# k and q of the last six steps transposed by DMA instead of TensorE

## The chip, the cores and the metric

The kernel runs on one core of one Trainium2 chip. Time is device microseconds (us) of one execution. Most executions of one kernel agree closely, but some fall into a slower state, a few per cent longer. Each run carries its state, "slow" when it is over 1.5% above the fastest run of the same kernel. A profiled execution has a span, from first to last instruction, which is about 1.8 us less than the run's time.

Engines: PE is TensorE, PEld its weight loads, DVE is VectorE, ACT is ScalarE, POOL is GpSimd, SP is SyncE. SPq and ACTq are the DMA issues of SyncE and ScalarE. L12 is line 12 of the kernel profiled, so the same statement has another line number in another kernel.

## The reference

```python
# attention with decay: B=4, H=8, S=768, D=64
intra = (q k^T * lam**(i-j) for i>=j) v                # inside a block
inter = (q * lam**(i+1)) @ state                        # what earlier blocks left
state = lam**block * state + (k * lam**(block-1-j))^T v
# then, on x = attention output as (B, S, 512):
h = relu(x @ w_in); u, v = halves of h (512 each)
v_n = (v - mean) / sqrt(var + 1e-6)
out = (u * (w_spatial @ v_n + b_spatial)) @ w_out
```

## The kernel before

There are 12 steps of 256 tokens (three per batch, numbered 0 to 11). For a step n the program has short names: `lk` loads k, q and v, `c` casts them on GpSimd, `T` transposes k and q, `A` computes the scores, `K` the new state, `O` the output of attention. `pv`, `pu`, `pvs`, `po` are the matmuls of the gated MLP (multilayer perceptron); batch 1's `pv` and `pu` run beside steps 5 to 7. The order on TensorE, GpSimd and SyncE is as written in the texts below. On ScalarE and VectorE a scheduler chooses it.

```python
def cast_part(s, n, part):
    if part == "k":      # product with the decay ldec: two inputs
        nc.gpsimd.tensor_tensor(out=kd..., in0=s["k_in"], in1=ldec..., op=ALU.mult)
    elif part == "q":    # plain cast
        nc.gpsimd.tensor_copy(out=qc..., in_=s["q_in"])
    ...
def trans_step(n):
    pt = two_banks([P, 2, NG, T2], f"pt_{n}", BF16)
    for j, src in ((0, kd), (1, qc)):
        for g in range(NG):
            for c in range(2):                      # 16 transposes of 128x128
                nc.tensor.transpose(out=pt[:, j, g, c * P:(c + 1) * P], in_=src..., identity=ident)
    nc.scalar.activation(out=kT, in_=pt[:, 0], func=AF.Copy)
    nc.vector.tensor_tensor(out=qT..., in0=pt[:, 1], in1=lq, op=ALU.mult)   # decay of q
...
def kv_step(n):                                     # the state; sd has two SBUF inputs
    nc.vector.tensor_tensor(out=sd, in0=prev, in1=lb, op=ALU.mult)
    nc.vector.tensor_tensor(out=s_sb[:, c], in0=sd, in1=pkv[:, c], op=ALU.add)
...
def pv(b, r):                                       # matmuls into ps, then
    nc.scalar.activation(out=vh[:, pair, :], in_=ps, func=AF.Relu)
    ... bn_stats, bn_aggr (VectorE), rstd (ScalarE), reciprocal, vn (VectorE)
...
run("""... c:5 lk:7 pvs:0:0 pvs:0:1 T:3 pvs:0:2 A:3 K:3 c:6 pvs:0:3 T:4 po:0:0
    A:4 O:3 K:4 po:0:1 c:7 po:0:2 lk:8 T:5 pv:1:0
    A:5 O:4 K:5 pu:1:0 lk:9 T:6 pv:1:1 pu:1:1""")
```

Of the kernel before, what the change touches and what calls it, by code (L numbers as in the profile page):

```python
# [9 lines left out]
FP32 = mybir.dt.float32  # L10
BF16 = mybir.dt.bfloat16
I32 = mybir.dt.int32  # L12
AF = mybir.ActivationFunctionType
ALU = mybir.AluOpType
# [4 lines left out]
def kernel(  # L19
# [12 lines left out]
    nc = tc.nc  # L32
    P = 128
    B, H, S, D = q.shape
# [4 lines left out]
    NG = H // 2  # L39
    NCH = DM // P  # L40
    NR = S // (2 * P)
    NS = B * NR
    T2 = 2 * P
    HW_ = S // 2

    const = ctx.enter_context(tc.tile_pool(name="const", bufs=1))
    wpool = ctx.enter_context(tc.tile_pool(name="wpool", bufs=1))
    fin = ctx.enter_context(tc.tile_pool(name="fin", bufs=4))
    att = ctx.enter_context(tc.tile_pool(name="att", bufs=3))
# [10 lines left out]
    st = {}  # L60

    def load_v(n, eng, blocks=(0, 1)):
        b, r = divmod(n, NR)
        toks = slice(r * T2, (r + 1) * T2)
        if "v_in" not in st[n]:
            st[n]["v_in"] = fin.tile([P, H, 2, D], FP32, tag="v_in", name=f"v_in_{n}")
        v_in = st[n]["v_in"]
        for c in blocks:
            eng.dma_start(out=v_in[:, :, c, :],  # L69
                          in_=v[b, :, toks][:, c * P:(c + 1) * P].rearrange("h p d -> p h d"))  # L70
# [32 lines left out]
    qpos_i = const.tile([P, 2, 2, D], I32)  # L103
    nc.gpsimd.iota(qpos_i, pattern=[[1, 2], [0, 2], [2, D]], base=1, channel_multiplier=0)

    rel_i = const.tile([P, 2, D], I32)
    nc.gpsimd.iota(rel_i, pattern=[[1, 2], [2, D]], base=0, channel_multiplier=-1)
    ident = const.tile([P, P], BF16)
# [3 lines left out]
    nc.vector.tensor_copy(out=krev, in_=krev_i)  # L112
    qpos = const.tile([P, T2], FP32)
    nc.vector.tensor_copy(out=qpos, in_=qpos_i.rearrange("p m a d -> p (m a d)"))
    causal = const.tile([P, P], FP32)
    nc.vector.tensor_scalar(out=causal, in0=rel_i.rearrange("p m d -> p (m d)"), scalar1=0,
                            scalar2=None, op0=ALU.is_ge)
# [5 lines left out]
    loglam = const.tile([P, H], FP32)  # L123
# [13 lines left out]
    with tc.issue_after(last.ins):  # L137
        load_v(0, nc.scalar, (1,))
        load_v(1, nc.scalar, (0,))
    l128 = const.tile([P, NG], FP32)  # L140
    nc.scalar.activation(out=l128, in_=logl, func=AF.Exp, scale=float(P))
    sq_t = const.tile([P, 1], FP32)
# [32 lines left out]
    def cast_step(n, parts=("k", "q", "v")):  # L175
        s = st[n]
        for part in parts:
            cast_part(s, n, part)

    def cast_part(s, n, part):  # L180
        if part == "k":
            kd = s["kd"] = att.tile([P, 2, H, D], BF16, tag="kd", bufs=4, name=f"kd_{n}")
            nc.gpsimd.tensor_tensor(out=kd.rearrange("p c h d -> p h c d"), in0=s["k_in"],  # L183
                                    in1=ldec.unsqueeze(2).unsqueeze(3).broadcast_to((P, H, 2, D)),
                                    op=ALU.mult)
        elif part == "q":
            qc = s["qc"] = att.tile([P, 2, H, D], BF16, tag="qc", bufs=4, name=f"qc_{n}")
            nc.gpsimd.tensor_copy(out=qc.rearrange("p m h d -> p h m d"), in_=s["q_in"])  # L188
        else:
            vc = s["vc"] = att.tile([P, H, 2, D], BF16, tag="vc", bufs=4, name=f"vc_{n}")  # L190
            nc.gpsimd.tensor_copy(out=vc, in_=s["v_in"])  # L191

    def trans_step(n):
        kd, qc = st[n]["kd"], st[n]["qc"]
        pt = two_banks([P, 2, NG, T2], f"pt_{n}", BF16)
        for j, src in ((0, kd), (1, qc)):
            for g in range(NG):
                for c in range(2):
                    nc.tensor.transpose(  # L199
                        out=pt[:, j, g, c * P:(c + 1) * P],  # L200
                        in_=src[:, c, 2 * g:2 * g + 2, :].rearrange("p h d -> p (h d)"),
                        identity=ident)
        kT = att.tile([P, NG, T2], BF16, tag="kT", name=f"kT_{n}")
        nc.scalar.activation(out=kT, in_=pt[:, 0], func=AF.Copy)  # L204
        qT = att.tile([P, NG, 2, 2, D], BF16, tag="qT", name=f"qT_{n}")
        nc.vector.tensor_tensor(out=qT.rearrange("p g m a d -> p g (m a d)"), in0=pt[:, 1],  # L206
                                in1=lq, op=ALU.mult)
        st[n]["qT"], st[n]["kT"] = qT, kT

    def qblk(n, g, hh, c):  # L210
        return st[n]["qT"][hh * D:(hh + 1) * D, g, :, c, :]

    def scores_step(n):


        kT = st[n]["kT"]
        a_sb = att.tile([P, 2, 2, 2, 2, P], BF16, tag="a_sb", bufs=2, name=f"a_{n}")
        st[n]["a"] = a_sb
        for i in range(2):
            pam = two_banks([P, 2, 2, 2, P], f"pam_{n}_{i}")  # L220
            for g2 in range(2):
                for c in range(2):
                    for hh in range(2):
                        g = 2 * i + g2
                        nc.tensor.matmul(out=pam[:, hh, g2, c, :],  # L225
                                         lhsT=kT[hh * D:(hh + 1) * D, g, c * P:(c + 1) * P],
                                         rhs=qblk(n, g, hh, c), start=True, stop=True)
            nc.vector.tensor_tensor(  # L228
                out=a_sb[:, i].rearrange("p h g c x -> p (h g) c x"),
                in0=pam.rearrange("p h g c x -> p (h g) c x"),  # L230
                in1=amask[:, i].rearrange("p h g x -> p (h g) x").unsqueeze(2)
                .broadcast_to((P, 4, 2, P)), op=ALU.mult)
# [143 lines left out]
    def wt_piece(s):  # L376
        ps = two_banks([P, 2, 1024], f"pwt_{s}", BF16)
        for j in range(2):
# [7 lines left out]
    acts = {"c": cast_step, "T": trans_step, "A": scores_step, "K": kv_step, "O": out_step,  # L386
            "lk": load_step, "pv": pv, "pu": pu, "pvs": pvs,
            "po": po, "wt": wt_piece, "win": load_win, "wsp": load_wsp, "wout": load_wout,
            "mask": make_amask, **{"c" + x: lambda n, x=x: cast_step(n, (x,)) for x in "kqv"}}

    def run(text):
        for word in text.split():
# [6 lines left out]
        T:0 K:0 A:0 T:1 O:0 K:1 A:1 pv:0:0 O:1 T:2 K:2 pv:0:1 A:2 pu:0:0 O:2  # L399
        c:4 pu:0:1 wt:0 pv:0:2 wt:2 pu:0:2 wt:4  # L400
        c:5 lk:7 pvs:0:0 pvs:0:1 T:3 pvs:0:2 A:3 K:3 c:6 pvs:0:3 T:4 po:0:0
        A:4 O:3 K:4 po:0:1 c:7 po:0:2 lk:8 T:5 pv:1:0
        A:5 O:4 K:5 pu:1:0 lk:9 T:6 pv:1:1 pu:1:1
    """)
    for n in range(2 * NR - 1, NS):
        b, r = divmod(n, NR)
        a = b - 1
        more = n + 1 < NS
        run((f"A:{n + 1} " if more else "") + f"O:{n}" + (f" K:{n + 1}" if more else ""))
        nxt = ""  # L410
        if n + 3 < NS:
            nxt += f" c:{n + 3}"
        if n + 5 < NS:
            nxt += f" lk:{n + 5}"
        if n + 2 < NS:
            nxt += f" T:{n + 2}"
        if n == 2 * NR - 1:
            run(f"pv:{b}:2 {nxt} pu:{b}:2")
        elif r == 0:
            run(f"pvs:{a}:0 pvs:{a}:1 {nxt} pvs:{a}:2 pvs:{a}:3")  # L420
        elif r == 1:
            run(f"po:{a}:0 po:{a}:1 {nxt} po:{a}:2 pv:{b}:0")
        elif more:
            run(f"pv:{b}:1 pu:{b}:0 pv:{b}:2 {nxt} pu:{b}:1 pu:{b}:2")
        else:
            run(f"pv:{b}:1 pv:{b}:2 pu:{b}:0 pu:{b}:1 pu:{b}:2")
# [31 lines left out]
```

## Time and profile before

The profile on which the prediction rests came from a run of 182.71 us, while the timed runs took 176.49 to 177.64.

| | profile of the slow run (used to predict) | profile of a fast run |
|---|---|---|
| span | 180.9 us | 174.4 us |
| scores of step 5 start | 74.79 | 72.67 |
| scores of step 7 start | 91.81, after a wait of 1.28 | 88.86, after a wait of 0.45 |
| scores of step 8 start | 108.23 | 101.70 |
| scores of step 8 to the end | 72.7 | 72.7 |

Two more places of the fast run will be needed, the first loads on SyncE and the first sd on VectorE:

```profile
0.74 1.07 SPq L78 DMA_DIRECT2D k_in<-in_k_dram  x2
1.86 1.12 SPq L80 DMA_DIRECT2D q_in<-in_q_dram  x1
```

```profile
17.36 1.94 DVE L254 TENSOR_TENSOR sd<-s,l 128x256 f32<-128x256 bf16 x1
...
91.63 0.72 DVE L325 TENSOR_SCALAR vn<-vh,mv,rstd 128x512 bf16<-128x512 bf16 x2
```

### The profile page before, as it was taken

What the parts mean: (1) busy time and instruction counts of PE and PEld (TensorE: products, weight loads), DVE (VectorE), ACT (ScalarE), POOL (GpSimd) and SP (SyncE); (2) the same over time, 40 slices, a digit from 0 to 9 for tenths busy, and PEclk for the clock granted to TensorE, in tenths of its full rate; (3) what the DMA queues carried; (4) which work ended last, traced back from release to release, by engine and by line L of the source; (5) the groups of instructions that cost most, each with busy time, mean ns of one, the idle gap of its engine ahead of it and who ended that gap; (6) DMA issues with size and microseconds to landing.
All of it is one profiled execution on the core that took longest, in us unless ns stands there. A gap on an engine that the chain in (4) does not pass through costs nothing.

```text
span 180.9 us, 3629 instructions
## 1 busy us (share of the span) xinstructions
PE 145.4 (80%) x1528; PEld 95.2 (53%) x1540; DVE 106.0 (59%) x182; ACT 77.3 (43%) x88; POOL 53.2 (29%) x50
## 2 busy tenths in 40 slices
PE   0041699399869999997955999999999999999890
PEld 0031566176636665676742655567866645776430
DVE  0712988921652889579998447179994713834400
ACT  2940057237911045677450014756822257660051
POOL 2439639400555566207556702000000000000000
PEclk9999999969987999999997899999999999999997
DMA  3999999999999999999899900630000026000036
GB/s 79 266 224 239 212 243 224 194 202 200 239 226 218 253 216 270 321 263 196 220 238 224 236 5 0 235 116 4 0 4 0 0 104 248 0 0 5 0 126 222
DMA packets 68497, 28.36 MB, mean 157 GB/s; under 512 B 50560, under 2 KB 65536, under 8 KB 68480
## 3 DMA queue, kind: packets, MB, share of 16 engines
q1 hardware_dynamic: 62560, 24.25, 58.2%
q0 software_dynamic: 2512, 2.95, 9.4%
q10 hardware_dynamic: 3408, 0.92, 2.7%
q8 instruction: 12, 0.20, 0.5%
q14 instruction: 5, 0.04, 0.1%
HBM read 24.78 MB, written 6.29 MB: 172 GB/s over the span
## 4 chain that ended last, share of the span: by engine, by line
PE 53%; DVE 17%; DMA 12%; SPq 9%; ACT 3%; issue 1%; POOL 1%; ACTq 0%; POOLq 0%
PE pvs L344 17%; PE po L359 10%; DMA wsp_raw<-in_moe_w_spatial_dram 8%; PE pv L313 8%; PE pu L334 7%; SPq L78 5%; DVE a L228 5%; DMA v_in<-in_v_dram 5%; DVE vn L325 4%; PE pvs L346 3%; PE pt L199 3%; DVE gT L348 2%; SPq L80 2%; DVE st L319 2%; SPq L69 2%; DVE sd L254 2%
## 5 line engine op out<-in xcount | busy, mean ns | idle before, releaser
L344 PE MATMUL pvs<-wt_sb,vn 128*128 128x384 bf16 x192 | 39.8, 343 | 5.2 <-DVE vn L325 5.1
L228 DVE TENSOR_TENSOR a<-pam,amask 128x1024 bf16<-128x1024 f32 x24 | 28.5, 1211 | 3.4 <-PE pam L225 3.4
L183 POOL TENSOR_TENSOR kd<-k_in,ldec 128x1024 bf16<-128x1024 f32 x12 | 23.0, 1917 | 23.2 <-DMA k_in<-in_k_dram 16.2
L344 PEld LDWEIGHTS <-vn 128*128 128x128 bf16 x192 | 19.4, 103 | 19.6 <-DVE vn L325 6.3
L204 ACT ACTIVATE kT<-pt 128x1024 bf16<-128x1024 bf16 x12 | 12.2, 1021 | 38.9 <-PE pt L199 38.9
L348 DVE TENSOR_TENSOR gT<-pvs,uT 128x768 bf16<-128x768 f32 x16 | 15.3, 957 | 19.6 <-PE pvs L346 19.6
L334 PE MATMUL pu<-xT,win_sb 128*128 128x256 bf16 x192 | 24.0, 284 | 2.9 <-DMA win_sb<-in_moe_w_in_dram 2.9
L313 PE MATMUL pv<-win_sb,xT 128*128 128x512 bf16 x89 | 22.0, 380 | 1.9 <-ACT xT L288 1.6
L359 PE MATMUL po<-wout_sb,gT 128*128 128x512 bf16 x91 | 21.7, 379 | 1.4 <-DVE a L228 0.7
L319 DVE BATCH_NORM_STATS2 st<-vh 128x6 f32<-128x512 bf16 x24 | 15.4, 682 | 12.5 <-ACT vh L316 12.3
L334 PEld LDWEIGHTS <-win_sb 128*128 128x128 bf16 x192 | 19.2, 102 | 6.6 <-DMA win_sb<-in_moe_w_in_dram 3.0
L288 ACT ACTIVATE xT<-pat 128x1024 bf16<-128x1024 f32 x12 | 15.8, 1320 | 15.6 <-PE pat L285 15.4
L191 POOL CAST vc<-v_in 128x1024 bf16<-128x1024 f32 x12 | 12.8, 1066 | 28.1 <-DMA v_in<-in_v_dram 20.9
L372 ACT ACTIVATE o<-po 128x1024 f32<-128x1024 f32 x11 | 11.3, 1025 | 18.3 <-PE po L359 18.3
L336 ACT ACTIVATE uT<-pu 128x1024 bf16<-128x1024 f32 x12 | 12.2, 1021 | 10.1 <-PE pu L334 10.1
L316 ACT ACTIVATE vh<-pv 128x1024 bf16<-128x1024 f32 x12 | 12.2, 1021 | 8.2 <-PE pv L313 8.1
L199 PE MATMUL pt<-ident,kd 128*128 128x128 bf16 x96 | 8.2, 234 | 9.1 <-POOL kd L183 9.1
L359 PEld LDWEIGHTS <-gT 128*128 128x128 bf16 x96 | 9.1, 98 | 11.7 <-DVE gT L348 1.3
L313 PEld LDWEIGHTS <-xT 128*128 128x128 bf16 x96 | 8.9, 98 | 11.3 <-ACT xT L288 2.0
L188 POOL CAST qc<-q_in 128x1024 bf16<-128x1024 f32 x12 | 12.9, 1076 | 5.9 <-DMA q_in<-in_q_dram 5.7
L206 DVE TENSOR_TENSOR qT<-pt,lq 128x1024 bf16<-128x1024 bf16 x12 | 8.2, 684 | 10.7 <-ACT kT L204 10.7
L325 DVE TENSOR_SCALAR vn<-vh,mv,rstd 128x512 bf16<-128x512 bf16 x24 | 14.1, 629 | 0.3
(54 smaller groups left out, 142.0 us busy)
## 6 DMA issues: line engine op xcount, KB each, us to landing
k_in<-in_k_dram SPq DMA_DIRECT2D x24, 256.0 KB, 5.3
q_in<-in_q_dram SPq DMA_DIRECT2D x12, 512.0 KB, 6.7
out_dram<-o SPq DMA_DIRECT2D x11, 512.0 KB, 3.1
v_in<-in_v_dram SPq DMA_DIRECT2D x21, 256.0 KB, 6.5
wsp_raw<-in_moe_w_spatial_dram POOLq DMA_DIRECT2D x1, 1152.0 KB, 14.2
win_sb<-in_moe_w_in_dram POOLq DMA_DIRECT2D x2, 512.0 KB, 8.2
v_in<-in_v_dram ACTq DMA_DIRECT2D x3, 256.0 KB, 6.3
wout_sb<-in_moe_w_out_dram POOLq DMA_DIRECT2D x1, 512.0 KB, 17.4
```

Source lines behind the costliest of these rows:

```text
L183: nc.gpsimd.tensor_tensor(out=kd.rearrange("p c h d -> p h c d"), in0=s["k_in"], in1=ldec.unsqueeze(2).unsqueeze(3).broadcast_to((P, H, 2, ...
L188: nc.gpsimd.tensor_copy(out=qc.rearrange("p m h d -> p h m d"), in_=s["q_in"])
L199: nc.tensor.transpose(out=pt[:, j, g, c * P:(c + 1) * P], in_=src[:, c, 2 * g:2 * g + 2, :].rearrange("p h d -> p (h d)"), identity=ident)
L228: nc.vector.tensor_tensor(out=a_sb[:, i].rearrange("p h g c x -> p (h g) c x"), in0=pam.rearrange("p h g c x -> p (h g) c x"), in1=amask[: ...
L288: nc.scalar.activation(out=xT[b][:, r].rearrange("p g (c d m) -> p (g c) m d", c=2, m=2), in_=po.rearrange("p g c (m d) -> p (g c) m d", m ...
L313: nc.tensor.matmul(out=ps[:, j], lhsT=x[:, r, c, j * P:(j + 1) * P], rhs=win_sb[:, c, DH:DFF], start=(c == 0), stop=(c == NCH - 1))
L319: nc.vector.bn_stats(out=m["st6"][:, t, :], in_=vh[:, t, :])
L325: nc.vector.tensor_scalar(out=m["vn"][:, t, :], in0=vh[:, t, :], scalar1=mv[:, t, 0:1], scalar2=rstd[:, t:t + 1], op0=ALU.subtract, op1=AL ...
L334: nc.tensor.matmul(out=ps[:, f], lhsT=win_sb[:, c, f * P:(f + 1) * P], rhs=x[:, r, c, :], start=(c == 0), stop=(c == NCH - 1))
L344: nc.tensor.matmul(out=ps[:, i, 0:HW_], lhsT=m["vn"][:, s, f * P:(f + 1) * P], rhs=wt_sb[:, s, cols], start=(s == 0), stop=False)
L348: nc.vector.tensor_tensor(out=m["gT"][:, f, :].rearrange("p (i x) -> p i x", i=2), in0=ps[:, :, 0:HW_], in1=m["uT"][:, f, :].rearrange("p ...
L359: nc.tensor.matmul(out=ps[:, j], lhsT=gT[:, c, t * P:(t + 1) * P], rhs=wout_sb[:, c, :], start=(c == 0), stop=(c == NCH - 1))
```

## The change

The intent: TensorE is the busiest engine, and 16 of its instructions a step only transpose. For steps 6 to 11 a DMA does it, from SBUF to SBUF, requested on SyncE's queue. The decay of q, which the removed VectorE product carried, moves into the q cast on GpSimd. kT and qT get five buffers instead of three.

```diff
+    NPE = 6
...
+    lqt = const.tile([P, 2, H], FP32)          # decay of q by token and head
...
-            nc.gpsimd.tensor_copy(out=qc..., in_=s["q_in"])
+            if n < NPE:
+                nc.gpsimd.tensor_copy(out=qc..., in_=s["q_in"])
+            else:
+                nc.gpsimd.tensor_tensor(out=qc..., in0=s["q_in"], in1=lqt..., op=ALU.mult)
...
+    def dma_trans(n):
+        kT = att.tile([P, 2, NG, P], BF16, tag="kT", bufs=5, name=f"kT_{n}")
+        qT = att.tile([P, 2, NG, P], BF16, tag="qT", bufs=5, name=f"qT_{n}")
+        for dst, src in ((kT, st[n]["kd"]), (qT, st[n]["qc"])):
+            nc.sync.dma_start_transpose(out=dst..., in_=src...)
...
     def trans_step(n):
+        if n >= NPE:
+            return
...
-        A:4 O:3 K:4 po:0:1 c:7 po:0:2 lk:8 T:5 pv:1:0
-        A:5 O:4 K:5 pu:1:0 lk:9 T:6 pv:1:1 pu:1:1
+        A:4 O:3 K:4 po:0:1 c:7 po:0:2 lk:8 dt:6 T:5 pv:1:0
+        A:5 O:4 K:5 pu:1:0 lk:9 dt:7 pv:1:1 pu:1:1
...
+        if n + 3 < NS:
+            nxt += f" dt:{n + 3}"              # behind lk:{n + 5}
```

More of the change, by code (lines that the diff above doesn't have):

```diff
@@ L104 @@
     nc.gpsimd.iota(qpos_i, pattern=[[1, 2], [0, 2], [2, D]], base=1, channel_multiplier=0)
+    tpos_i = const.tile([P, 2], I32)
+    nc.gpsimd.iota(tpos_i, pattern=[[1, 2]], base=1, channel_multiplier=2)
     rel_i = const.tile([P, 2, D], I32)
@@ L114 @@
     nc.vector.tensor_copy(out=qpos, in_=qpos_i.rearrange("p m a d -> p (m a d)"))
+    tpos = const.tile([P, 2], FP32)
+    nc.vector.tensor_copy(out=tpos, in_=tpos_i)
+    nc.vector.tensor_scalar(out=tpos[D:P, :], in0=tpos[D:P, :], scalar1=-float(P), scalar2=None,
+                            op0=ALU.add)
     causal = const.tile([P, P], FP32)
@@ L139 @@
         load_v(1, nc.scalar, (0,))
+    lqt = const.tile([P, 2, H], FP32)
+    with tc.issue_after(last.ins):
+        for m in range(2):
+            nc.scalar.activation(out=lqt[:, m, :], in_=loglam, func=AF.Exp,
+                                 scale=tpos[:, m:m + 1])
     l128 = const.tile([P, NG], FP32)
@@ L187, in cast_part @@
             qc = s["qc"] = att.tile([P, 2, H, D], BF16, tag="qc", bufs=4, name=f"qc_{n}")
-            nc.gpsimd.tensor_copy(out=qc.rearrange("p m h d -> p h m d"), in_=s["q_in"])
+            if n < NPE:
+                nc.gpsimd.tensor_copy(out=qc.rearrange("p m h d -> p h m d"), in_=s["q_in"])
+            else:
+                nc.gpsimd.tensor_tensor(out=qc.rearrange("p m h d -> p h m d"), in0=s["q_in"],
+                                        in1=lqt.rearrange("p m h -> p h m").unsqueeze(3)
+                                        .broadcast_to((P, H, 2, D)), op=ALU.mult)
         else:
@@ L191, in cast_part @@
             nc.gpsimd.tensor_copy(out=vc, in_=s["v_in"])
+    def dma_trans(n):
+        kT = att.tile([P, 2, NG, P], BF16, tag="kT", bufs=5, name=f"kT_{n}")
+        qT = att.tile([P, 2, NG, P], BF16, tag="qT", bufs=5, name=f"qT_{n}")
+        for dst, src in ((kT, st[n]["kd"]), (qT, st[n]["qc"])):
+            nc.sync.dma_start_transpose(out=dst.rearrange("p c g x -> p (c g) x"),
+                                        in_=src.rearrange("p c h d -> p (c h d)"))
+        st[n]["qTd"], st[n]["kTd"] = qT, kT
     def trans_step(n):
+        if n >= NPE:
+            return
         kd, qc = st[n]["kd"], st[n]["qc"]
@@ L202, in trans_step @@
                         identity=ident)
-        kT = att.tile([P, NG, T2], BF16, tag="kT", name=f"kT_{n}")
+        kT = att.tile([P, NG, T2], BF16, tag="kT", bufs=5, name=f"kT_{n}")
         nc.scalar.activation(out=kT, in_=pt[:, 0], func=AF.Copy)
-        qT = att.tile([P, NG, 2, 2, D], BF16, tag="qT", name=f"qT_{n}")
+        qT = att.tile([P, NG, 2, 2, D], BF16, tag="qT", bufs=5, name=f"qT_{n}")
         nc.vector.tensor_tensor(out=qT.rearrange("p g m a d -> p g (m a d)"), in0=pt[:, 1],
@@ L208, in trans_step, with kblk @@
         st[n]["qT"], st[n]["kT"] = qT, kT
+    def kblk(n, g, hh, c):
+        if n >= NPE:
+            return st[n]["kTd"][hh * D:(hh + 1) * D, c, g, :]
+        return st[n]["kT"][hh * D:(hh + 1) * D, g, c * P:(c + 1) * P]
     def qblk(n, g, hh, c):
+        if n >= NPE:
+            return st[n]["qTd"][hh * D:(hh + 1) * D, :, g, c * D:(c + 1) * D]
         return st[n]["qT"][hh * D:(hh + 1) * D, g, :, c, :]
     def scores_step(n):
-        kT = st[n]["kT"]
         a_sb = att.tile([P, 2, 2, 2, 2, P], BF16, tag="a_sb", bufs=2, name=f"a_{n}")
@@ L225, in scores_step @@
                         nc.tensor.matmul(out=pam[:, hh, g2, c, :],
-                                         lhsT=kT[hh * D:(hh + 1) * D, g, c * P:(c + 1) * P],
+                                         lhsT=kblk(n, g, hh, c),
                                          rhs=qblk(n, g, hh, c), start=True, stop=True)
@@ L388 @@
             "po": po, "wt": wt_piece, "win": load_win, "wsp": load_wsp, "wout": load_wout,
-            "mask": make_amask, **{"c" + x: lambda n, x=x: cast_step(n, (x,)) for x in "kqv"}}
+            "mask": make_amask, "dt": dma_trans, **{"c" + x: lambda n, x=x: cast_step(n, (x,)) for x in "kqv"}}
     def run(text):
```

## The prediction

> **What bounds the kernel now.** I read the share of each engine first, then the slices, then the waits of TensorE, and then the order of time around the places where the changed steps are used. The profiled run took 180.9 us, the timed ones 177.02; I work in the profile's clock and carry only the difference over to the timed run.
>
> ```profile
> PE 145.4 (80%) x1528; PEld 95.2 (53%) x1540; DVE 106.0 (59%) x182; ACT 77.3 (43%) x88; POOL 53.2 (29%) x50
> ...
> PE   0041699399869999997955999999999999999890
> ...
> DMA  3999999999999999999899900630000026000036
> ```
>
> TensorE (PE) is busy in nine tenths of each slice from about 100 us on, and nothing is loaded there. From 5 to 103 us the DMA engines are full. So there are two stages: until about 100 us loads, VectorE (DVE) and TensorE take turns; after it TensorE alone sets the time, and each microsecond taken from it there is one off the end. The change touches both: steps 6 and 7 are used in the first stage, steps 8 to 11 in the second.
>
> The timeline shows what 16 TensorE transposes of a step really cost:
>
> ```profile
> 87.72 0.61 PE L199 MATMUL pt<-ident,kd 128*128 128x128 bf16 x8
> 88.17 0.61 PE L199 MATMUL pt<-ident,qc 128*128 128x128 bf16 x8
> 88.62 1.91 PE L334 MATMUL pu<-xT,win_sb 128*128 128x256 bf16 x16
> ```
>
> Columns are start and length. From 87.72 to 88.62 is 0.90 us for 16, or 56 ns each; the 219 ns duration of one is mostly pipeline. At 102.69, 113.92, 125.52 and 136.34 the same 0.90 us recurs.
>
> The queue of SyncE (SP), which issues nearly all loads and will issue the transposes, is the view that decides the rest:
>
> ```profile
> 68.47 4.99 SPq L373 DMA_DIRECT2D out_dram<-o  x3
> 73.55 1.88 SPq L78 DMA_DIRECT2D k_in<-in_k_dram  x2
> 75.52 1.52 SPq L80 DMA_DIRECT2D q_in<-in_q_dram  x1
> 77.13 3.44 SPq L69 DMA_DIRECT2D v_in<-in_v_dram  x2
> 80.67 2.70 SPq L78 DMA_DIRECT2D k_in<-in_k_dram  x2
> ...
> 88.20 2.51 SPq L78 DMA_DIRECT2D k_in<-in_k_dram  x2
> ...
> 94.23 2.50 SPq L78 DMA_DIRECT2D k_in<-in_k_dram  x2
> ```
>
> These are the loads of steps 8 (from 73.55), 9 (80.67), 10 (88.20) and 11 (94.23). SP is occupied without a gap, about 7 us per step, and whatever stands behind a load waits for it.
>
> **What the Trainium skill says.** "DMA: Bandwidth & Descriptors", section "Latency and other measured facts", gives a DMA transpose 261 GB/s: for our 256 KB that makes an estimate of 1.0 us of transfer. The section "Anatomy of one DMA" adds about 2 us fixed. No transpose by DMA is in this trace; its nearest relative is a 256 KB half of k, which takes 1.2 to 1.4 us on SP's queue and lands 5.3 us (median) after issue when the engines are full, while an output store later, on idle engines, takes 3.1. The section "Issuing engines are not separate DMA queues" says all transfers share the same 16 engines, so I take the landing of a k load, not 3 us, for those transposes that are issued among loads. "TensorE: Matmul & The Clock Gate", "Part 4: PE-mode transpose", gives about 275 ns for a transpose; here the pace is 56 ns, so the trace decides. "SBUF — State Buffer", "Who interferes with whom", says that a VectorE instruction with two SBUF inputs, or in a two-port mode, and a GpSimd one that reads SBUF exclude each other. The trace agrees: sd takes 0.43 us in the median and 1.95 beside GpSimd's k cast at 86.82, and the two vn at 94.58 take 2.84 instead of 0.73.
>
> **The change part by part.** *Removed:* six times 16 transposes, 6 x 0.90 = 5.4 us of TensorE; six kT copies of ScalarE (ACT), 6 x 1.02 = 6.1 us; six qT products of VectorE, 6 x 0.68 = 4.1 us. ScalarE and VectorE lie mostly beside TensorE. One wait on VectorE goes too: the scores of step 7 waited 1.28 us for qT at 91.81. *Added:* 12 DMA transposes of 256 KB (3 MB); six q casts become products with a second input, like the k cast (1.90 us instead of 1.04), 5.2 us of GpSimd (POOL), which has room (29% busy), but which hold VectorE up a little longer. The constants at the start cost nothing on the path.
>
> *Moved, by the built order.* Two things that the diff hides. First, SP's order: the transposes of step 6 stand behind all loads of step 8, those of step 7 behind step 9's, and so on; those of step 10 even behind two output stores. So they are not requested when GpSimd has cast them (step 6 was cast at 65.2) but when SP gets to them. Second, the scheduler has changed the order on ScalarE and VectorE around step 5, which the change doesn't name: the vh eviction and rstd of the first block of batch 1 now stand ahead of kT of step 5 on ScalarE, and bn_stats to vn ahead of qT of step 5 on VectorE. TensorE's order there is the same as before (transposes of 5, the pv product, scores of 5), so the scores of 5 now wait for the whole chain.
>
> The ledger, as slips against the time before:
>
> Scores of step 5, at 74.79 before. pv ends about 74.6; vh 1.02, two bn_stats 1.28, aggregates 0.3, rstd 0.3, kT 1.0 beside vn 0.73, qT 0.69: start at about 79.4, slip **+4.6**.
>
> Scores of step 6, at 82.82 before. 8.03 us lie between, less 0.90: TensorE is ready at 86.5. The transposes: SP reaches them at 80.6; two issues of 1.2 us end at 83.0; landing 4 to 5 us later, 87. Slip **+4.2**: the late transfer is largely hidden behind the first slip.
>
> Scores of step 7, at 91.81 before. 8.99 us lie between, less 0.90 and the 1.28 wait: ready at 93.8. SP: 83.0, then step 9's loads (7.4), then two issues: 92.8, landed at about 97. Slip **+5.2**, a wait of 3.2 us.
>
> Scores of step 8, at 108.23 before: slip 5.2 - 0.9 = **+4.3**, at 112.5; its transposes are issued by 92.8 + 6.0 + 2.4 = 101.2 and landed by 106. From here no transfer is late: step 9 by 114 against 121.8, and steps 10 and 11, issued after the stores of batch 1 at some 114 to 119, ten and more us before use. Steps 9, 10 and 11 give 0.9 each: **+1.6** at the end.
>
> The sum: 4.6 + 0.5 + 3.2 of waits, less 5.4 and 1.28, is +1.6 us: 177.0 becomes about 178.5.
>
> **The rivals.** *TensorE's 5.4 us all come off:* the simple reading, 171.6, 3% faster. For it: TensorE is the busiest engine and the last 80 us are its own. Against it: the two waits, which come before that stage and aren't caught up by anything but the removed work itself. It needs the scheduler's order to be harmless and the transfers of steps 6 and 7 to land within some 2 us. If only step 7's wait is absent, 175.3. *The transpose is much slower than a copy:* if each held SP and the engines 4 us instead of 1.2, step 6 would land at about 92 (80.6 + 8 + 3 or more) and step 7 at 107 (80.6 + 8 + 7.4 + 8 + 3), a slip of 15 there; step 8's loads-and-transposes cycle of 14 us would keep up with TensorE's, so some 12 stays: 188. For it: neither its time on SP nor at the engines is in this trace. *Loads become the bound:* 3 MB more for full DMA engines, and SP seven instead of five issues a step. The loads of step 11 would land some 7 us later than 100, yet are used at 141.9: slack of 30 us, so nothing. *The longer GpSimd casts hold VectorE:* each 0.86 us more can delay one sd or vn; the wait of 2.1 us for vn at 96.44 shows such a delay on the path. At most 1 or 2 us more, 180.
>
> **Range and chances.** Centre 178.5. Below it, 175.3 if step 7 isn't late and 171.6 if nothing is; above it, 180 with the cast effect and 188 for a slow transpose. I take 172 to 186. The gain by over 2% (under 173.5) needs both waits to be wrong: 0.18. Over 2% slower (over 180.6) needs a transpose of some 2 us on SP or a worse order: 0.32. Within 2%: 0.50.
>
> **What would show it.** In the changed profile: TensorE's own busy time falls by about 5 us; the scores of step 5 wait some 4 us for qT from VectorE, behind vn; those of step 6 wait little and those of step 7 some 3 us for a DMA of kT or qT; no score from step 8 on waits for one; SP shows transposes of about 1.2 us each behind the loads; qc by a two-input product takes 1.9 us. After 112 us the slip shrinks by 0.9 a step. I'm wrong if the scores of 5 start near 75 (the order mattered less), if a transpose takes above 2 us on SP or lands later than 6 us, or if the loads feed the casts too late in steps 9 to 11.

## More of the kernel before

A later profile of the kernel before is from a fast run of 176.17 us. Of the fast run's page, the busy times and the slices of TensorE and of its granted clock:

```profile
PE 141.8 (81%) x1540; PEld 93.6 (54%) x1540; DVE 98.7 (57%) x182; ACT 77.3 (44%) x88; POOL 52.9 (30%) x50
...
PE   0041489579969989999788999999999999999980
...
PEclk9999999978999999999999999999999999999999
```

The clock is at nine tenths or more in nearly every slice. The score matmuls in its timeline (start, length, engine, line, operation, and in brackets the idle time ahead with what ended it), of steps 3, 5, 7 and 8:

```profile
57.72 0.62 PE L225 MATMUL pam<-qT,kT 64*128 64x128 bf16 x16
...
72.67 0.62 PE L225 MATMUL pam<-qT,kT 64*128 64x128 bf16 x16 [0.17 <-DVE qT L206]
...
88.86 0.62 PE L225 MATMUL pam<-qT,kT 64*128 64x128 bf16 x16 [0.45 <-DVE qT L206]
101.70 0.62 PE L225 MATMUL pam<-qT,kT 64*128 64x128 bf16 x16
```

These starts are the ruler of this document: a slip is the difference of such a start between two kernels.

## The result, and the profile after

The changed kernel took 184.14 us (median of four runs, 183.00 to 187.78, the longest of them slow) against 177.33 for the kernel before in the same rounds. The ratio is 1.037, with a 95% interval of 1.030 to 1.044: slower. Here and below a ratio is the mean time of one kernel's fast runs over that of the other's of the same rounds, so not quite the ratio of the quoted medians.

The profile of after is from a fast run (184.4 us, span 182.6), so it is compared with the fast profile of before: 8.2 us more. The same lines of its page:

```profile
PE 139.7 (77%) x1432; PEld 90.7 (50%) x1444; DVE 105.3 (58%) x178; ACT 72.1 (39%) x84; POOL 58.5 (32%) x51
...
PE   0041069798969969459976699999999999999890
...
PEclk9999999999999999956999799999999999999998
```

TensorE has only 2.1 us less to do by this sum (12 of its 1444 matmuls are missing from the trace), where 5.4 was expected, and the clock line shows the main reason: a new dip to 5 and 6 tenths in slices 18 and 19, from 78 to 87 us. The scores of steps 5, 7 and 8, with the first pu behind the scores of 5:

```profile
79.69 1.04 PE L259 MATMUL pam<-qT,kT 64*128 64x128 bf16 x16 [4.67 <-DVE qT L234]
...
82.86 3.11 PE L368 MATMUL pu<-xT,win_sb 128*128 128x256 bf16 x16
...
97.40 0.62 PE L259 MATMUL pam<-qT,kT 64*128 64x128 bf16 x16 [1.22 <-DMA qT<-qc]
...
112.52 0.62 PE L259 MATMUL pam<-qT,kT 64*128 64x128 bf16 x16
```

The scores of 5 wait 4.67 us for qT from VectorE. Then 16 of them take 1.04 us where 0.62 is usual, and pu 3.11 where 1.91 is usual: the granted clock is 0.50 from 79.6 to about 85.3. The 4.67 us are the chain that the scheduler moved ahead, here on ScalarE and on VectorE:

```profile
75.12 1.02 ACT L350 ACTIVATE vh<-pv 128x1024 bf16<-128x1024 f32 x1 [1.65 <-PE pv L347]
77.71 0.29 ACT L355 ACTIVATE rstd<-mv,eps_t 128x2 f32<-128x2 f32 x1 [1.57 <-DVE mv L354]
77.91 1.00 ACT L232 ACTIVATE kT<-pt 128x1024 bf16<-128x1024 bf16 x1
```

```profile
78.24 0.73 DVE L359 TENSOR_SCALAR vn<-vh,mv,rstd 128x512 bf16<-128x512 bf16 x2
78.95 0.69 DVE L234 TENSOR_TENSOR qT<-pt,lq 128x1024 bf16<-128x1024 bf16 x1
...
100.17 2.30 DVE L359 TENSOR_SCALAR vn<-vh,mv,rstd 128x512 bf16<-128x512 bf16 x2
```

The transposes had been finished on TensorE since 73.14. The last line is the other late spot: vn beside a GpSimd cast takes 2.30 us, where the fast profile of before has 0.72. SyncE's queue, the transposes of steps 6 and 7:

```profile
79.49 2.94 SPq L215 DMA_TRANSPOSE kT<-kd  x1
82.61 2.26 SPq L215 DMA_TRANSPOSE qT<-qc  x1
...
90.12 2.56 SPq L215 DMA_TRANSPOSE kT<-kd  x1
92.86 1.23 SPq L215 DMA_TRANSPOSE qT<-qc  x1
```

And the start, where nothing was expected: the first load of q on SyncE, the first sd on VectorE, and GpSimd's casts beside it:

```profile
1.87 2.34 SPq L81 DMA_DIRECT2D q_in<-in_q_dram  x1
```

```profile
18.75 4.76 DVE L288 TENSOR_TENSOR sd<-s,l 128x256 f32<-128x256 bf16 x1
```

```profile
18.36 1.05 POOL L202 CAST qc<-q_in 128x1024 bf16<-128x1024 f32 x1
19.34 1.05 POOL L209 CAST vc<-v_in 128x1024 bf16<-128x1024 f32 x1
20.35 1.90 POOL L196 TENSOR_TENSOR kd<-k_in,ldec 128x1024 bf16<-128x1024 f32 x1
22.20 1.03 POOL L202 CAST qc<-q_in 128x1024 bf16<-128x1024 f32 x1
```

The q load takes 2.34 us on the queue instead of 1.12. Everything behind it comes later, so that GpSimd's casts follow each other without a gap from 18.36 to 23.23. The sd that starts at 18.75 ends only when they do, at 23.5. Before, the casts paused at 19.0 for k of step 2, and sd was through in 1.94 us.

The slips, start of scores against the fast profile of before:

| scores of step | predicted slip | measured slip | piece since the row above: predicted, measured |
|---|---|---|---|
| 3 | 0 | +1.7 | 0, +1.7 |
| 5 | +4.6 | +7.0 | +4.6, +5.4 |
| 6 | +4.2 | +8.7 | -0.4, +1.7 |
| 7 | +5.2 | +8.5 | +1.0, -0.1 |
| 8 | +4.3 | +10.8 | -0.9, +2.3 |
| end | +1.6 | +8.2 | -2.7, -2.6 |

### The profile page after: what moved, and what is told of

Read it like the earlier page. It is cut to its first block, busy times and chain, and to the rows that moved or that the text cites. A ratio compares the mean times of both kernels' runs of the same rounds, so it can differ in the third digit from the quotient of the medians.

```text
span 182.6 us, 3455 instructions
## 1 busy us (share of the span) xinstructions
PE 139.7 (77%) x1432; PEld 90.7 (50%) x1444; DVE 105.3 (58%) x178; ACT 72.1 (39%) x84; POOL 58.5 (32%) x51
## 4 chain that ended last, share of the span: by engine, by line
PE 50%; DVE 33%; DMA 4%; ACT 4%; SPq 3%; issue 2%; POOL 2%; ACTq 0%; POOLq 0%; DVEq 0%
PE pvs L378 16%; PE po L393 10%; DVE a L262 9%; PE pv L347 7%; DVE sd L288 6%; PE pu L368 6%; DVE st L353 5%; DVE vn L359 5%; DMA k_in<-in_k_dram 4%; PE pvs L380 3%; DVE gT L382 2%; PE pat L319 2%; PE pt L227 2%; SPq L79 2%; ACT vh L350 2%
## 5 line engine op out<-in xcount | busy, mean ns | idle before, releaser
L378 PE MATMUL pvs<-wt_sb,vn 128*128 128x384 bf16 x192 | 38.5, 335 | 4.4 <-DVE vn L359 2.4
L259 PE MATMUL pam<-qT,kT 64*128 64x128 bf16 x192 | 8.7, 239 | 12.9 <-DVE qT L234 11.6
L288 DVE TENSOR_TENSOR sd<-s,l 128x256 f32<-128x256 bf16 x16 | 16.9, 1059 | 0.5
L232 ACT ACTIVATE kT<-pt 128x1024 bf16<-128x1024 bf16 x6 | 6.1, 1018 | 27.7 <-PE pt L227 27.7
L393 PEld LDWEIGHTS <-gT 128*128 128x128 bf16 x96 | 9.1, 98 | 12.8 <-DVE gT L382 2.2
L259 PEld LDWEIGHTS <-kT 64*128 64x128 bf16 x192 | 6.7, 105 | 16.2 <-issue 11.7
L359 DVE TENSOR_SCALAR vn<-vh,mv,rstd 128x512 bf16<-128x512 bf16 x24 | 13.3, 596 | 0.3
```

The source lines that it names most:

```text
L359: nc.vector.tensor_scalar(out=m["vn"][:, t, :], in0=vh[:, t, :], scalar1=mv[:, t, 0:1], scalar2=rstd[:, t:t + 1], op0=ALU.subtract, op1=AL ...
L378: nc.tensor.matmul(out=ps[:, i, 0:HW_], lhsT=m["vn"][:, s, f * P:(f + 1) * P], rhs=wt_sb[:, s, cols], start=(s == 0), stop=False)
L393: nc.tensor.matmul(out=ps[:, j], lhsT=gT[:, c, t * P:(t + 1) * P], rhs=wout_sb[:, c, :], start=(c == 0), stop=(c == NCH - 1))
```

## The experiments

Twelve kernels ran. Where "before" is the base of an edit, it is the kernel before; otherwise it is the changed kernel. `issue_after` holds an instruction behind another in its engine's order.

### b0_before: the kernel before, unchanged

> The kernel before, unchanged, to have a profile of it in the fast state (the first one was taken in a slow run, 182.7 us). All theories expect 176.5 to 178 us. What it tells: if its span is near 175, the scores of steps 5 to 8 must start some 5 us earlier than in the slow profile (74.8, 82.8, 91.8, 108.2), and the place where the slow profile lost these 5 us is to be seen in the TensorE clock; if they start at the same places, the 5 us lie after 108 us.

Its profiled run was fast: 176.17 us, span 174.4. A second run took 181.78 and was slow. So the kernel before falls into a state some 5 us longer on its own, and the profile used to predict was of it. Its lines are shown above.

### e_force: the change, with the old order around step 5

```diff
-        nc.scalar.activation(out=vh[:, pair, :], in_=ps, func=AF.Relu)
+        if (b, r) == (1, 0):
+            with tc.issue_after(kT_of_step_5):
+                nc.scalar.activation(out=vh[:, pair, :], in_=ps, func=AF.Relu)
```

> The change with the order on ScalarE and VectorE around step 5 put back (kT of step 5 ahead of vh of the first block of batch 1, qT ahead of bn_stats); nothing else moves. Theory 1 (order and late transposes both cost, and hide each other): the scores of 5 start at about 75.5 instead of 79.7, the scores of 6 then wait 3 to 5 us for the transpose of step 6, so only 1 to 4 us come back: 180 to 183. Theory 2 (the order is the whole loss): 175 to 177, faster than before by up to 2%. Theory 3 (the order costs nothing, the transposes and the casts do): 183 to 185, unchanged.

Measured: 183.16 us against 177.56, ratio 1.030 (1.021 to 1.039). The scores of 5 come at 76.22 after a wait of 0.17 us, 3.5 us earlier than in the change. Those of 6 and 7:

```profile
87.75 1.03 PE L259 MATMUL pam<-qT,kT 64*128 64x128 bf16 x16 [2.65 <-DMA qT<-qc]
...
97.32 0.62 PE L259 MATMUL pam<-qT,kT 64*128 64x128 bf16 x16 [1.50 <-DMA qT<-qc]
```

Once the wait for the order is gone, the wait for the transfer shows in its place, and the clock halves behind it too. By step 7 the 3.5 us have shrunk to 0.1; at the end of the profiles 1.7 are left (180.9 against 182.6). The two faults lay over each other, as the prediction had it; the time is just above the 180 to 183 of theory 1. The order alone isn't the cause of the loss.

### b_order: the kernel before, with only the new order around step 5

```diff
-        nc.scalar.activation(out=kT, in_=pt[:, 0], func=AF.Copy)
+        with tc.issue_after(rstd_of_pv_1_0):          # step 5 only
+            nc.scalar.activation(out=kT, in_=pt[:, 0], func=AF.Copy)
-        nc.vector.tensor_tensor(out=qT..., in0=pt[:, 1], in1=lq, op=ALU.mult)
+        with tc.issue_after(vn_of_pv_1_0):            # step 5 only
+            nc.vector.tensor_tensor(out=qT..., in0=pt[:, 1], in1=lq, op=ALU.mult)
```

> The kernel before with only that new order forced on it (vh and rstd of the first block of batch 1 ahead of kT of step 5 on ScalarE, bn_stats to vn ahead of qT of step 5 on VectorE), transposes all on TensorE. Theory 1 and 2: the scores of 5 wait 4 to 5 us, TensorE's clock drops after the wait, and the end comes 5 to 7 us later: 182 to 184. Theory 3: the delay is absorbed by later slack, within 2 us of before: 177 to 179.

Measured: 184.85 us, ratio of fast runs 1.040 (1.032 to 1.048), so some 7 us. The profiled run was slow (190.49 us), so only its order is read and not its times against a fast one; the wait is there:

```profile
81.12 0.62 PE L240 MATMUL pam<-qT,kT 64*128 64x128 bf16 x16 [4.66 <-DVE qT L215]
```

In a kernel that has no other fault, this order alone costs as much as the whole change did, and more than its own wait of 4.66 us. Behind the wait TensorE's clock falls here too (granted 0.50 from 82 to 85 us); what else the rest is made of a slow profile doesn't settle. In the change most of it is covered by the late transposes, as e_force shows.

### b_cast: the kernel before, with only the longer q casts

Steps 6 to 11 cast q with the decay on GpSimd. They are still transposed by TensorE, and VectorE multiplies by ones. The constants of the change are made too.

```diff
+                nc.gpsimd.tensor_tensor(out=qc..., in0=s["q_in"], in1=lqt..., op=ALU.mult)   # n >= 6
...
-                                in1=lq, op=ALU.mult)
+                                in1=lq if n < NPE else ones, op=ALU.mult)
```

> The kernel before with only the casts of the change: q of the last six steps is cast by a two-input product on GpSimd, and the product on VectorE that evicts qT multiplies by ones, so that its cost stays. Theory 1: 6 x 0.9 us more of GpSimd, of which one or two hold up an sd or vn on the path: 0.5 to 2 us, 177.5 to 179. Rival: GpSimd has room and VectorE is not held on the path: 177.0 to 177.5. Rival: the casts explain what the ledger lacks, 4 to 5 us: 181 to 182.

Measured: 180.06 us, ratio 1.015 (1.010 to 1.020), about 2.6 us and more than theory 1 allowed. The scores of 3 come at 56.34, 1.4 us earlier than in the fast profile of before. From there it loses 2.0 us up to the scores of 4 (they wait 1.75 us for qT, behind a sd of 2.04 us), 1.3 up to 5 (the scores of 4 run at 1.04 us), 0.7 between 6 and 7 and 1.5 between 7 and 8, where vn takes 2.22 us instead of 0.72. But the first longer q cast starts at 64.44. The sd of 2.04 us (from 62.47) ended just as that cast started; it ran beside a k cast, as did vn, and k casts are as long as before (1.9 us). So the edit costs 2.6 us, and the profile shows casts that coincide with an sd or vn. That their greater length does it is not shown here.

### x_one: only step 11 by DMA

```diff
-    NPE = 6
+    NPE = 11
```

> The changed kernel with only the last step (11) transposed by DMA and cast by the two-input product; all other steps as before. In the fast profiles the changed kernel and e_force both start the scores of step 0 at 24.6 us, the kernel before and b_cast at 20.0 to 20.5, with the first q load 2.34 instead of 1.12 us on SyncE's queue. Theory 1: a program with a DMA transpose has this later start whatever its number, so scores of 0 at about 24.6, +1.7 by the scores of 3 and -0.9 at step 11: 177.5 to 179. Rival: the later start comes from something else in the six-step version; then scores of 0 at 20 to 20.5 and 176 to 177.5.

Measured: 181.21 us against 178.57, ratio 1.018 (1.006 to 1.030). Two transposes, near 117 us, for whose results no score waits, and yet the loss is there from the start: the first q load takes 2.32 us, and the scores of 0 come at 24.55 instead of 19.95, those of 3 at 60.09 instead of 57.72. So a fault sits in the program as built and not in the traffic of the transposes. x_act takes it up.

### x_plain: e_force with plain q casts (a wrong result)

```diff
-            if n < NPE:
-                nc.gpsimd.tensor_copy(...)
-            else:
-                nc.gpsimd.tensor_tensor(...)
+            nc.gpsimd.tensor_copy(out=qc..., in_=s["q_in"])
```

> e_force with the plain one-input q casts put back for all steps; the decay of q is then missing for the last six steps and the result is wrong on purpose. The order of all instructions is the same as in e_force. Theory 1: the two-input casts hold VectorE (sd and vn) on the path also here, so 2 to 4 us come back: 179 to 181 against 183.2. Rival: with the transposes late anyway the casts hide beside their wait: 182 to 183.5.

Measured: 183.94 us, ratio 1.037 (1.026 to 1.049); the result is wrong, as q lacks its decay. In e_force a sd of 1.17 us at 66.26 ran beside a longer q cast; here that sd takes 0.42. The scores of 5 come at 74.59 instead of 76.22, but those of 6 then wait 3.05 us for the DMA instead of 2.65. At the end nothing is gained (181.3 against 180.9). The shorter casts do gain that time, and while SyncE's queue sets the pace of step 6 they are worth nothing.

### e_early: the transposes ahead of the loads on SyncE

```diff
-        A:4 O:3 K:4 po:0:1 c:7 po:0:2 lk:8 dt:6 T:5 pv:1:0
-        A:5 O:4 K:5 pu:1:0 lk:9 dt:7 pv:1:1 pu:1:1
+        ... c:6 pvs:0:3 T:4 dt:6 po:0:0
+        A:4 O:3 K:4 po:0:1 c:7 po:0:2 T:5 dt:7 lk:8 pv:1:0
+        A:5 O:4 K:5 pu:1:0 lk:9 pv:1:1 pu:1:1
```

and `dt` ahead of `lk` in the loop. The scheduler then keeps the old order around step 5 by itself.

> The change with the transposes of each step placed right behind its casts on SyncE's queue, ahead of the loads that stood before them (and with the scheduler's order around step 5 as in the kernel before, as it comes out of this text). Theory 1: the scores of 6 and 7 no longer wait for a DMA (4.1 us in e_force, plus the slow clock after it), and loads two steps ahead bear the delay: 178 to 180.5. Rival: SyncE now stands waiting for the casts with the loads behind it, casts of 8 to 11 come later and scores of 8 or 9 wait instead: 182 to 185.

Measured: 181.89 us, ratio 1.025 (1.015 to 1.035). No score waits for a DMA any more: those of 6 start at 83.45 and of 7 at 90.19, against 89.38 and 97.40. But those of 8 start at 108.83, 18.6 us later, where before it was 12.8. VectorE, with the same work, meets GpSimd's casts there. On VectorE and TensorE:

```profile
95.97 2.76 DVE L359 TENSOR_SCALAR vn<-vh,mv,rstd 128x512 bf16<-128x512 bf16 x2
```

```profile
97.75 0.34 PE L378 MATMUL pvs<-wt_sb,vn 128*128 128x384 bf16 x1 [2.02 <-DVE vn L359]
```

With waits for s and a (1.35 and 1.42) and for the second vn (0.70) that makes 5.5 us, of which the kernel before has 0.7 (its own wait for the second vn). Against e_force, which has the same order around step 5, the scores of 7 come 7.1 us earlier and those of 8 only 2.0. What the earlier transfers gave up to step 7 is largely lost at the next place where TensorE depends on VectorE.

### e_late: steps 8 to 11 by DMA, 6 and 7 by TensorE

```diff
-    NPE = 6
+    NPE = 8
-        A:4 ... lk:8 dt:6 T:5 pv:1:0
-        A:5 ... lk:9 dt:7 pv:1:1 pu:1:1
+        A:4 ... lk:8 T:5 pv:1:0
+        A:5 ... lk:9 T:6 pv:1:1 pu:1:1
```

> The change for the last four steps (8 to 11) alone, steps 6 and 7 on TensorE and cast plainly; the scheduler's order around step 5 is as before. Theory 1: no score waits for a DMA and 4 x 0.9 = 3.6 us of TensorE come off; against it the later start (+1.7) and some of the cast effect (0 to 2): 175 to 177.5, within 2% of before. Rival: the removed transposes are not on the path at all, and only the costs stay: 179 to 181.

Measured: 180.14 us, ratio 1.012 (1.000 to 1.024). The order around step 5 is the old one; the new order has moved to step 7, now the last by TensorE:

```profile
93.74 0.62 PE L259 MATMUL pam<-qT,kT 64*128 64x128 bf16 x16 [3.38 <-DVE qT L234]
```

In both kernels the scheduler puts the evictions of the last step transposed on TensorE behind the block beside them. From the scores of 8 (106.21) no score waits, and the last stage takes 70.3 us instead of 72.7, short of three times 0.9 by 0.3. So the time is the rival's, but not its reason: the removed transposes do come off.

### e_order2: e_force, with the first state copy held behind qT of step 0

In the change both copies of the state s stand ahead of qT of step 0 on VectorE; in e_late and x_plain too. The text below takes the first copy for the difference. By the traces it isn't: in the kernel before, the first s (16.83) and the first sd stand ahead of that qT (19.22) too, and only the second s (19.82) behind it. So the edit makes an order that neither kernel had.

```diff
-                nc.vector.tensor_copy(out=s_sb[:, c], in_=pkv[:, c])
+                with tc.issue_after(qT_of_step_0):            # step 0 only
+                    nc.vector.tensor_copy(out=s_sb[:, c], in_=pkv[:, c])
```

> The change with the order around step 5 restored (as in e_force) and now also the first state copy s of step 0 held behind qT of step 0 on VectorE, as in the kernel before. Theory (the later first loads set the start: k of step 1 is cast while the first sd is due, and GpSimd's back-to-back casts hold that sd for some 4.8 us): qT of step 0 is no longer delayed, so the scores of 0 start near 21, but their eviction still stands behind the held sd, so the scores of 1 and 2 stay near 29 and 38; the time is within 0.5 us of e_force's, ratio about 1.030. Rival (the order of s ahead of qT is what delays the start): scores of 0 near 20, of 2 near 33, of 3 near 58, some 2 us off the end, ratio about 1.018.

Measured: 183.59 us against 177.21, ratio 1.034 (1.028 to 1.041), no different from e_force. The scores of 0 come at 18.11, earlier than the 21 expected. But sd is still held, 4.83 us from 18.67, and the scores of 3 start at 60.33, as in e_force (60.19). The order at step 0 isn't the fault. x_act below says the same more directly: it has the change's order there and starts early. One more line, for the clock: here the scores of 6 wait as long as in e_force and run at full pace.

```profile
87.87 0.62 PE L259 MATMUL pam<-qT,kT 64*128 64x128 bf16 x16 [2.63 <-DMA qT<-qc]
```

### e_best: e_late, with the old order at step 7 and the edit of e_order2

```diff
+            with tc.issue_after(kT_of_step_7):                # pv of block (1, 2) only
+                nc.scalar.activation(out=rstd..., func=AF.Sqrt, ...)
+            with tc.issue_after(second_a_of_step_7):
+                nc.vector.reciprocal(out=rstd[:, pair], in_=rstd[:, pair])
...
+            with tc.issue_after(kT_of_step_7):                # pu of block (1, 2) only
+                nc.scalar.activation(out=uT..., in_=ps, func=AF.Relu)
```

The reciprocal and vn are also written behind the scores of 7, and the edit of e_order2 is in.

> e_late (steps 8 to 11 by DMA, 6 and 7 by TensorE) with the order around step 7, its last step by TensorE, put back as in the kernel before (kT and qT of 7 ahead of rstd, reciprocal and vn of the block beside it), and with s of step 0 behind qT of step 0. Theory (whichever step is the last by TensorE has its evictions put behind the block beside it, and that order costs about 3 us): the scores of 7 start at about 90.8 instead of 93.7 without the 3.4 us wait, four times 0.9 us come off after it, and the profile ends at about 173.5, ratio 0.99 to 1.00, so even with or a little faster than the kernel before. Rival (the wait was only a cover for late vn or casts, which now show themselves): the scores of 8 start no earlier than 105.5, end 176, ratio 1.01.

Measured: 175.64 us against 177.21, ratio 0.991 (0.985 to 0.996). By the limit of 2% that is the same, but the interval lies below 1, and it is the only variant that does so. The scores of 7 and 8:

```profile
91.32 0.62 PE L259 MATMUL pam<-qT,kT 64*128 64x128 bf16 x16 [0.65 <-DVE qT L234]
...
104.12 0.62 PE L259 MATMUL pam<-qT,kT 64*128 64x128 bf16 x16
```

The wait fell from 3.38 to 0.65 us, and the scores of 7 come 2.4 us earlier than in e_late. The span, 174.4, is 0.9 above what was expected and no shorter than that of before: the profiled run, 176.23 us, was the longest of the five fast ones (from 174.20), so the gain is seen in the times and not in this pair of profiles. Between 7 and 8 nothing is gained (12.8 us, as in the kernel before, though 16 transposes are gone), because pvs waits 0.83 and 0.70 us for vn, where before it waited 0.69 once. The rival, that the wait was only a cover, fell: 2.1 of its 2.4 us arrive at step 8.

### x_act: x_one, with the transposes issued by ScalarE

```diff
-            nc.sync.dma_start_transpose(...)
+            nc.scalar.dma_start_transpose(...)
```

> x_one (only step 11 by DMA) with its two transposes issued on ScalarE's queue instead of SyncE's. It tells whether the later first loads belong to the queue that carries a transpose or to the program that has one. Theory (the program): nothing changes at the start, first q load still 2.3 us on SyncE, scores of 0 at 24.6, ratio about 1.018. Rival (the queue): first q load 1.1 us again, first bytes half a microsecond to one earlier, scores of 0 near 20, ratio about 1.005. ScalarE gives some 3 us for the issues near 117 us, beside TensorE's work; no score waits for it.

Measured: 176.76 us, ratio 0.997 (0.992 to 1.003), against x_one's 1.018. My theory fell: the late start belongs to SyncE's queue with transposes on it, and not to the program. The first q load on SyncE is short again:

```profile
1.86 1.04 SPq L81 DMA_DIRECT2D q_in<-in_q_dram  x1
```

sd takes 1.93 us again, and the scores of 0 and 3 come at 20.35 and 57.32, as before. The kernel differs from x_one's only in which engine issues the two transposes; VectorE and GpSimd run the same instructions in the same order in both traces. That any queue would start late with a transpose on it isn't shown: ScalarE's has them here, and its first v load takes 0.61 us, against 0.62 in the kernel before.

### e_act: e_best, with the transposes issued by ScalarE

```diff
-            nc.sync.dma_start_transpose(...)
+            with tc.issue_after(xT_of_step_6):       # steps 8, 9, 10; xT_of_step_9 for 11
+                nc.scalar.dma_start_transpose(...)
```

> e_best with its eight transposes (steps 8 to 11) issued on ScalarE's queue: those of 8, 9 and 10 one after the other behind the xT copy of step 6, where ScalarE idles from about 94 to 106 us in e_best, those of 11 behind the xT copy of step 9, near 127. Theory (the slow first loads belong to the queue that carries a transpose): first q load on SyncE near 1.1 us, scores of 1 near 25 instead of 27.2, of 3 near 57.3 instead of 59.4, of 7 near 89.3; the transposes of 8 land by about 102, so the scores of 8 wait at most 1 us; then three times 0.9 and the end at 172.3 in the profile; ratio 0.975 to 0.985, the fastest of all. Rival (ScalarE, held by transposes that wait for casts, delays the xT copy of step 7 and the stores behind it): the start is the same, but the scores of 9 come at 113 or later as in e_best, end 174.5, ratio about 0.99.

Measured: 178.22 us against 177.29, ratio 1.005 (0.997 to 1.013). Neither the theory's time nor the rival's way to it. The start came off as expected: first q load 1.14 us, scores of 3 at 56.40. The profiled run was slow (179.72 us, the fastest 176.81), so the rest is read with care. In it the scores of 7 come 10.1 us after those of 6 (2.40 of it a wait for qT, and then at 1.04 us), and those of 8 a further 16.5 us later, where e_best needed 8.4 and 12.8. ScalarE wasn't late: the xT copy of step 7, the next on it, started at 109.39 behind the scores of 8 and 3.8 us after its last transpose issue. VectorE was late:

```profile
94.55 2.92 DVE L377 TENSOR_SCALAR vn<-vh,mv,rstd 128x512 bf16<-128x512 bf16 x2
```

GpSimd's casts, with their loads from a faster start, ran from 87.06 to 91.03 beside an sd of 2.04 us and from 93.49 to 97.32 beside this vn. How much of that a fast run of e_act has stays open.

## Why the prediction was right or wrong

**The removed work: right.** Six times 0.90 us of TensorE were counted. From the scores of 8 to the end the slip shrinks by 2.6 us (0.90, 0.89, 0.53 and 0.3 from one step to the next and to the end), where 2.7 was predicted; no score waits for a DMA there. This part of the gain is real, and it is what e_best lives on.

**Scores of step 5: the mechanism right.** "kT 1.0 beside vn 0.73, qT 0.69": each duration of the chain was met within 0.1 us, and the wait is 4.67. The piece from the scores of 4 to those of 5 is 4.5 us, where 4.6 was predicted. The other 2.5 us of the slip of 7.0 had come before: 1.7 up to the scores of 3, and 0.9 up to those of 4, where a sd took 1.27 us beside a k cast of usual length (the first longer q cast began at 64.10, as this sd ended).

**"The constants at the start cost nothing on the path": true of the constants, but a cost of the start was missed.** b_cast and x_act have the constants without the loss. x_one has the loss with only two transposes, and x_act loses it again when another queue carries them. By these two ratios (1.018 over 0.997, each against the kernel before in its own rounds, on different chips) it is some 2.1%, about 3.7 us. In their profiles it is 2.8 us at the scores of 3. In the change it is smaller at that point, 1.7. This is the first step that failed.

**Scores of step 6: the wait right, the clock missed.** "The late transfer is largely hidden behind the first slip" holds: in the change the scores of 6 don't wait, and in e_force, where the first slip is gone, they wait 2.65 us. But the piece from 5 to 6 is +1.7 instead of -0.4. Less 0.9 for the transposes it should have been -0.9, and the half clock behind the 4.67 us wait added 2.6. The prediction counted a wait as its own length. The Trainium skill, "TensorE: Matmul & The Clock Gate", "Part 1: The HAM clock gate (the "warmup" mystery)", says that the clock falls to half after an idle window of about 3.4 us and comes back after about as long a time of work. I had read the page for the cost of a transpose and not for this. This trace agrees in kind: 16 score matmuls at 1.04 us against 0.62 behind the wait. The full clock came back at about 85.3, 5.6 us after the work began, so later than the page says.

**Scores of step 7: right in kind, too large.** A wait of 3.2 us for DMA was predicted, 1.22 measured. The transfers were as late as worked out or later: SyncE was done with the transposes of 7 at 94.1 (92.8 predicted), and qT arrived at 97.4 (97). But TensorE was itself ready only at 96.2 instead of 93.8, and so waited less. The wait of 1.28 us for qT, which the prediction credited here, is 0.45 in a fast run, so most of it couldn't be earned. A transpose held SyncE for 1.23 to 2.94 us, not 1.2, and landed after 5.5 (kT) and 4.1 (qT) in the median, where 4 to 5 were assumed. Six of the twelve were above the 2 us on SP that the prediction named as a sign of being wrong, and one kT landed after 6.2; this part of the sum was mis-sized, though little of it shows as a wait here.

**Scores of step 8: wrong by 3.2 us.** Predicted -0.9, measured +2.3. What came is this, on GpSimd and on TensorE:

```profile
100.26 2.07 POOL L196 TENSOR_TENSOR kd<-k_in,ldec 128x1024 bf16<-128x1024 f32 x1 [4.95 <-DMA k_in<-in_k_dram]
```

```profile
102.53 0.50 PE L378 MATMUL pvs<-wt_sb,vn 128*128 128x384 bf16 x1 [1.56 <-DVE vn L359]
```

vn took 2.30 us beside this k cast, and pvs waited 0.69 and 1.56 us for it. The first of these waits is in the fast run of before too. The second, and the half clock behind it until about 105.8, are some 1.6 us each, together the 3.2. The rival of the prediction, "the longer GpSimd casts hold VectorE", is near this but isn't shown by it: the cast is a k cast, hardly longer than before, and it came at this moment because it had waited 4.95 us for its load. In the fast run of before the k casts started at 88.71 and 95.16 and missed vn at 91.63. b_cast measures its edit as 2.6 us alone, against "at most 1 or 2 us", but most of its loss too lies beside casts of the old length.

**The sum.** The errors of the pieces: 2.4 up to step 5 for the start and a held sd, 2.1 at step 6 for the clock, -1.1 at step 7, 3.2 at step 8, together the 6.6 that the end is off (8.2 less 1.6). In time, 184.14 against 178.5 lies inside the range of 172 to 186, and "slower" had a chance of 0.32. The range held for reasons that the prediction didn't have: its high end was a slow transpose.

There is a second way to read the same error. In the clock of the slow profile, in which the ledger was worked out, its times came true within half a microsecond, but for the scores of 6 (89.38 against 87, the clock): scores of 5 at 79.69 (79.4 predicted), of 7 at 97.40 (97), of 8 at 112.52 (112.5), the end at 182.6 (180.9 + 1.6). What failed is the step "I work in the profile's clock and carry only the difference over to the timed run": the base of that difference was 182.71 us and not 177.0. That the ledger met these times is in part luck. The slow profile had a late start of its own (scores of 3 at 60.23, in the change 59.38) and its own vn beside a k cast (2.84 us; 16.4 us from the scores of 7 to those of 8), just where the change in its fast state has such losses and the fast kernel before has not.

**What stays open.** Why SyncE's first loads are slower when the program has a transpose on its queue further down. How much of the cast effect is the casts' length and how much the moment at which they fall. And whether order, late transfer and cast effect add up to the rest, as each was tried alone and they overlap: the order costs 7 us alone and about 1 in the change.

## What to carry to other kernels

Before a profile serves as a baseline, compare its run's time with the timed runs: a slow one hands you waits that a fast one doesn't have, and their removal earns nothing. When an operation moves to a DMA, look at the order on the engines that you didn't touch, above all for the last step still done the old way, and at the first loads of the queue that gets the new transfers (SyncE's were slower here, ScalarE's were not). Work taken off the busiest engine counts only where nothing else is late: here the last three steps gave their 0.9 us each, and the variant that kept the DMA to steps 8 to 11, with the order held, was the only one whose interval lies below the kernel before.

## What the Trainium skill lacked or had wrong

- No page has it: SyncE's queue starts its loads more slowly when it carries a DMA transpose later in the program. The first q load took 2.32 to 2.36 us on SyncE with transposes there (x_one, the change, e_best) and 1.04 to 1.14 with none there (the kernel before, x_act, e_act). It cost some 2.1% in x_one. ScalarE's queue didn't show it: its first v load took 0.61 us with transposes on it (x_act, e_act) and 0.62 without (the kernel before).
- "DMA: Bandwidth & Descriptors", "Latency and other measured facts": its 261 GB/s gives an estimate of 1.0 us for 256 KB, and the section has no time on the issuing queue. Here one held SyncE's queue for 1.23 to 2.94 us and landed after 5.5 us (kT) and 4.1 (qT) in the median of the change; the two of step 11 in x_act, issued by ScalarE, took 4.6 and 4.2.
- "SBUF — State Buffer", "Who interferes with whom": it says that the two engines exclude each other for an instruction. It lacks that a row of casts without a gap holds a VectorE instruction for several of them: sd took 4.76 us beside four casts, and 0.43 alone.
- "TensorE: Matmul & The Clock Gate", "Part 1": the clock also fell behind shorter waits than the 3.4 us it names: 1.03 us for 16 score matmuls after a wait of 2.65 (e_force), while after 2.63 (e_order2) they ran at 0.62 and so did what followed. After 3.38 (e_late) the first 16 ran at 0.62, and the clock fell just behind them (granted 0.50 from 95 to 98 us). A wait of 2 to 3 us may or may not cost more than its length.
